# One recurrence, one MLP, one core: an audit of the inputs moved, and a chunk's vector work laid out in other slots

## The chip, the cores and the metric

The kernel runs on one core of a Trainium2 chip. The time is device microseconds of one launch, the median of several runs. The engines are named as in the profile: PE (matrix products), PEld (its weight loads, which overlap), DVE (vector), ACT (scalar functions and copies), POOL (GpSimd), SP (issues the transfers). Each engine takes its instructions in one fixed order; an instruction waits in place for what it needs, and all behind it on that engine wait too.

## The reference

A gated linear recurrence (4 batches, 8 heads, 768 tokens, head size 48), then an MLP with SiLU over the 3072 tokens (384 to 2048 to 384). Attention is float32; the weights come as 64-bit floats, whose bits the kernel converts:

```python
for t in range(S):
    state = alpha[:, :, t, :, None] * state + np.einsum('bhd,bhe->bhde', k[:, :, t], v[:, :, t])
    y[:, :, t] = np.einsum('bhd,bhde->bhe', q[:, :, t], state)
x = y.transpose(0, 2, 1, 3).reshape(B * S, H * D)
h = x @ w_in
out = (h / (1 + np.exp(-h))) @ w_out
```

## The kernel before

**Chunks.** The recurrence is done in chunks of 128 tokens: NT = 24 chunks, n = 0 to 23, four batches for each of six positions in the sequence. Within a chunk it becomes matrix products: with the running products of alpha, k is multiplied by the decay from its token to the chunk's end (`u`, then `kp`), q by the inverse of that (`p`, then `qp`), and scores are masked products of both. A chunk has four stages:

- `products(n)`, lines 648 to 691: alpha, k and q are turned so that the head's dimension lies on the partitions. For the first NA = 8 chunks PE does that (line 669); later DVE does it, with 32x32 transposes (lines 654 to 656) from one set of three tiles ("quads") that twelve transfers fill (lines 461 to 468). DVE scans alpha backwards (line 674), multiplies k (681), takes the chunk's whole decay `c["all"]`, bounds and inverts it (683, 684), scans forwards (686, into `p`, of which there are two) and multiplies q (691).
- `scores(n)`, 693 to 715: PE's scores (702), masked by DVE (706); k is turned back by PE (710) and copied by ACT (712) for the state; from the second position on, DVE multiplies the batch's state by the chunk's decay (715).
- `values(n)`, 720 to 740: y from scores and v, and from q and the state (735), copied by ACT into `xt` (740).
- `states(n)`, 741 to 756: the chunk's addition to the state (PE, 748), summed by DVE (754) or copied at the first position (756). The last position needs none.

The PSUM results of these stages come from one pool of three buffers, `ps_attn()`; 710, 735, 748 and 702 take turns in it.

**The MLP in pieces.** It runs over groups of four chunks (512 tokens), NG = 6. Groups 0 and 1 go through a plain input layer (`enter_plain`, line 791); groups 2 to 5 through `enter` (814), which forms 20 products of sums in place of 24: DVE makes sums of inputs (`sums_x`, eleven per group, 546 to 551) and once sums of weights (`sums_w`, the same lines, made between the pieces of the two output layers named in line 954), ACT copies and applies SiLU (820, 825), DVE combines (828). The output layer (`leave`, 912; 939 for the first one) does seven products in place of eight, with subtractions on DVE (917), sums (926, 977, 979, 988) and stores on SP (928). A generator yields after each piece; a piece of `enter` is twelve matmul records of PE, one of `leave` sixteen. The list `pieces` (1023 to 1040) holds 173 entries in the order in which they are to run, those of a group's input layer in turn with those of the output layer of the group before it.

**The audit** (611 to 640). The scheme holds only for inputs within certain bounds, so the kernel reads alpha (9 transfers of 1024 columns) and the bits of both weight matrices (12 transfers of 512, 16 of 384) a second time, reduces each on DVE (639: one reduction for alpha, two for a weight tile, 65 in all) and compares at the end (1111 to 1125). The generator has one buffer, `look`: a call reduces what the call before it loaded, then issues the next load. If the verdict `within` fails, a general kernel runs behind it (line 1156); all engines load the verdict (1128) and branch.

**What sets the order.** The program is written out by loops of 25 steps of four slots (1086 to 1106): in a slot one stage of one chunk, then `fill`, which calls the audit and runs pieces until the work that is due at that slot is done. A step lasts about as long as PE needs for its pieces. From step 4 on the slots are: scores of the chunk before, products of this chunk, values and states of the chunk before. `load(n + 2)` for the quads stands behind the states. In `fill` the audit is called at every slot while groups 0 and 1 are the ones at work (`i < 2`), at every third slot afterwards: its 37 tiles are all called for by the end of step 24. `settle` (1058) sets up the later chunks' tiles at the end of step 7's second slot.

The written order is a priority, not the last word: a planner orders each engine's instructions by when it expects them to be ready, and the written order decides between those that are. `tc.keep_in_program_order` pins an instruction behind the one that stands ahead of it on its engine in the text; the audit's reductions and the sums of weights are pinned so. Behind attention, 39 of the 173 pieces are left.

Of the kernel before, what the change touches and what calls it, by code (L numbers as in the profile page):

```python
# [8 lines left out]
F32 = mybir.dt.float32  # L9
# [4 lines left out]
ALU = mybir.AluOpType  # L14
# [341 lines left out]
def quotients(  # L356
# [20 lines left out]
    pe, dve, act, gps = nc.tensor, nc.vector, nc.scalar, nc.gpsimd  # L377
    B, H, S, D = q.shape
    C = 128
    NCH = S // C  # L380
    NP = H // 2
# [4 lines left out]
    NT = B * NCH  # L386
    W = C + 1
# [7 lines left out]
    def pool(name, bufs=1, space=None):  # L395
        kw = {} if space is None else {"space": space}
        return ctx.enter_context(tc.tile_pool(name=name, bufs=bufs, **kw))
# [17 lines left out]
    def out_bank(i, n):  # L415
        return outs[i].tile([128, 512], F32, name="ps_o")[:, 0:n]

    def ps_attn(n=C):
        return ps_a.tile([128, 512], F32, name="ps_a").rearrange("p (j c) -> p j c", c=n)
# [18 lines left out]
    NA = 2 * GB  # L438
# [8 lines left out]
    ctxs = {}  # L447

    def load(n):
        c = ctxs.setdefault(n, dict(zip(("ci", "b"), divmod(n, B))))  # L450
        b, rows = c["b"], slice(c["ci"] * C, c["ci"] * C + C)
        for name, src in (("a", alpha), ("k", k), ("q", q)):
            x = src[b, :, rows, :]
            if n < NA:
                c[name] = nat[name][n % NIN]
                nc.sync.dma_start(c[name][:, :, 0:D], x.transpose([1, 0, 2]))
                continue

            c[name] = late["quads"][name]
            for u in range(2):
                for i in range(2):
                    r = 64 * u + 32 * i
                    nc.sync.dma_start(  # L465
                        c[name][r : r + 32, 32 * (1 - i) :][:, 0 : 4 * NP * D].rearrange(
                            "p (g c) -> p g c", g=NP),
                        x[u::2].rearrange("h (b j) d -> b h (j d)", j=4))

    NV = 2  # L470
# [4 lines left out]
    def load_v(n):  # L475
        c = ctxs.setdefault(n, dict(zip(("ci", "b"), divmod(n, B))))
        rows = slice(c["ci"] * C, c["ci"] * C + C)
        t = c["v"] = vns[n % NV]
        nc.sync.dma_start(t[:, :, 0:D], v[c["b"], :, rows, :].transpose([1, 0, 2]))
# [23 lines left out]
    seg = [(fix if i == 0 else spare).tile([128, NP * W + 1], F32, name=f"al{i}") for i in range(2)]  # L503
    inv = fix.tile([128, NP * W + 1], F32, name="inv")
# [137 lines left out]
    xts, xcs, late = {}, {}, {}  # L642

    def tokens(t):

        return t[:, 1 : NP * W + 1].rearrange("p (j c) -> p j c", c=W)[:, :, 0:C]

    def products(n):

        c = ctxs[n]  # L650
        sg, iv = seg[0 if late else n % 2], inv
        ps = {}

        def turned(name, to):
            x = c[name][:, 32:].rearrange("p (g j d) -> p g j d", j=4, d=D)
            dve.transpose(to.rearrange("p g (b j) -> p g j b", j=4), x[:, :, :, 0:32])  # L656

        for name in ("a", "k", "q"):
            if n >= NA:
                if name == "a":  # L660
                    turned(name, tokens(sg))
                continue
            if n < GB and name != "a":

                ps[name] = out_bank("kq".index(name), 512).rearrange("p (j c) -> p j c", c=C)
            else:
                ps[name] = ps_attn()
            for j in range(NP):
                pe.transpose(ps[name][:, j, :], c[name][:, 2 * j : 2 * j + 2, :], ident)
            if name == "a":  # L670
                act.copy(tokens(sg), ps[name])  # L671
        end = NP * W
        u = upool.tile([128, end + 1], F32, name="u")
        dve.tensor_tensor_scan(u[:, end - 1 :: -1], sg[:, end:0:-1], one[:, end:0:-1],  # L674
                               0.0, ALU.mult, ALU.add)

        kp = c["kp"] = u[:, 1 : end + 1].rearrange("p (j c) -> p j c", c=W)[:, :, 0:C]
        if n >= NA:
            ps["k"] = late["turn"].tile([128, NP, C], F32, name="turn")
            turned("k", ps["k"])  # L680
        dve.tensor_tensor(kp, ps["k"], kp, ALU.mult)
        c["all"] = u[:, 0:end:W]
        dve.tensor_single_scalar(least[:, n, :], c["all"], 2.0**-64, ALU.max)
        dve.reciprocal(iv[:, 0:end:W], least[:, n, :])
        p = ppool.tile([128, end + 1], F32, name="p")
        dve.tensor_tensor_scan(p[:, 0:end], sg[:, 0:end], iv[:, 0:end], 0.0, ALU.mult, ALU.add)  # L686
        qp = c["qp"] = tokens(p)
        if n >= NA:
            ps["q"] = late["turn"].tile([128, NP, C], F32, name="turn")
            turned("q", ps["q"])  # L690
        dve.tensor_tensor(qp, ps["q"], qp, ALU.mult)

    def scores(n):
        c = ctxs[n]
        ci, b = c["ci"], c["b"]
        ps = [ps_attn() for _ in range(2)]


        for j in range(NP):
            for u in range(2):  # L700
                r = slice(64 * u, 64 * u + D)
                pe.matmul(ps[u][:, j, :], lhsT=c["kp"][r, j, :], rhs=c["qp"][r, j, :],  # L702
                          start=True, stop=True)
        g = c["g"] = work.tile([128, 2, NP, C], F32, name="g")
        for u in range(2):
            dve.tensor_tensor(g[:, u], ps[u], mask[:, None, :].to_broadcast([128, NP, C]), ALU.mult)  # L706
        if ci < NCH - 1:
            ps_k = ps_attn()
            for j in range(NP):
                pe.transpose(ps_k[:, j, :], c["kp"][:, j, :], ident)  # L710
            c["kn"] = work.tile([128, NP, C], F32, name="kn")
            act.copy(c["kn"], ps_k)
        if ci > 0:
            s = st[b].rearrange("p j u e -> p j (u e)")
            dve.tensor_tensor(s, s, c["all"][:, :, None].to_broadcast([128, NP, 2 * D]), ALU.mult)

# [58 lines left out]
    turn = [0, 1, 2]  # L777
# [267 lines left out]
    def go_on():  # L1045

        nonlocal done
        next(pieces[done][0], None)
        done += 1
# [8 lines left out]
    def settle():  # L1058

        first.close()  # L1060
        late.update(look=pool("look"), part=pool("part"), xc=pool("xc"), turn=pool("turn"),
                    wx=pool("wx").tile([128, 8, NQ, 128], F32, name="wx"))
        quads = pool("quads")
        late["quads"] = {name: quads.tile([128, 32 + 4 * NP * D], F32, name=f"{name}t") for name in "akq"}
        for name, t in late["quads"].items():
            gps.memset(t, 1.0 if name == "a" else 0.0)
        load(NA)

    def fill(step, slot):

        at = step * SLOTS + slot
        if at < marks[0]:
            if step >= 1:
                convert(0, (at - SLOTS) * 3 // (marks[0] - SLOTS) + 1)
            return
        i = next(i for i, m in enumerate(marks[1:]) if at < m)
        a, b = [work_at[n] for n in ([0] + phases)[i : i + 2]]
        due = a + (b - a) * (at - marks[i] + 1) / (marks[i + 1] - marks[i])
        if late and (i < 2 or at % 3 == 0):
            next(audits, None)  # L1080
        while work_at[done + 1] <= due and pieces[done][2] <= bridged:
            convert(0, 3 * (done // 2) + 6)
            convert(1, 3 * (done - 6) // 2)
            go_on()

    for step in range(STEPS):
        stages = ((scores, 1), (products, 0), (values, 1), (states, 1))
        if step < GB:

            stages = stages[1::-1] + stages[2:]  # L1090
        for slot, (stage, lag) in enumerate(stages):
            n = step - lag
            if 0 <= n < NT:
                stage(n)
                if stage is values:
                    bridged = n + 1
                if stage is products and n + NIN < NA:
                    load(n + NIN)
                if stage is states:
                    if NA < n + 2 < NT:  # L1100
                        load(n + 2)
                    if n + NV < NT:
                        load_v(n + NV)
            fill(step, slot)
            if step >= NA - 1 and slot > 0 and conv_done[1] == NFT and not late:
                settle()
    while next(audits, 0) is None:
        go_on()
        go_on()

    checks = [(least.rearrange("p n j -> p (n j)"), ALU.min, 2.0**-64, ALU.is_gt),
              (seen[0][0], ALU.max, 1.0, ALU.is_le)]
# [10 lines left out]
    ps = ps_attn()[0:1, 0, 0:1]  # L1123
# [64 lines left out]
```

## Time and profile before

| | |
|---|---|
| median of 3 runs | 599.41 us (599.15 to 600.26) |
| the profiled execution | 599.32 us |
| its span, first to last instruction | 597.5 us |
| PE busy in it | 570.7 us (96%) |
| DVE busy | 464.0 us (78%) |
| ACT busy | 162.5 us (27%) |
| POOL busy | 7.3 us (1%) |
| moved by DMA | 63.69 MB, 107 GB/s |

Times below and in the prediction are microseconds from the start of the span. A line of the groups gives the source line, the engine, what is written from what, and the count, then busy time and the mean of one in ns, then the engine's idle time ahead of it and what ended that. In a timeline a line is a start and a duration, and in brackets the idle time ahead of it with what ended it. A matmul of float32 is two records of the trace. `seen` is the audit's result, `bits` its buffer (and that of the weights' conversion earlier on), `st` a state, `g` the hidden layer as well as the scores.

### The profile page before, as it was taken

The numbers are of one execution on the slowest core, as the hardware profiler recorded it, in microseconds if no ns is written. First come the engines' busy times: TensorE is split into PE (matmuls) and PEld (weight loads), VectorE is DVE, ScalarE is ACT, GpSimd is POOL, SyncE is SP. The second block draws the span as 40 slices with busy tenths as digits, with TensorE's granted clock in tenths as the row PEclk, the third lists the DMA queues.
The fourth block names the chain that finished last, engine by engine and source line by source line (L and its number), as shares of the span: only waits on it lengthen the run. The fifth ranks groups of instructions, "written<-read, shape, count | busy, mean of one in ns | idle before, by whom it ended". The sixth has DMA issues, their size and how long they took to land.

```text
span 597.5 us, 10662 instructions
## 1 busy us (share of the span) xinstructions
PE 570.7 (96%) x4290; PEld 505.0 (85%) x4290; DVE 464.0 (78%) x835; ACT 162.5 (27%) x279; POOL 7.3 (1%) x25
## 2 busy tenths in 40 slices
PE   5899999988999979989999999999999999999996
PEld 4677887667889868869899999999999998999996
DVE  6889898869999889999699898799794473635531
ACT  2244442011211113123233224223232242342200
POOL 4000000000000000000000000000000000000000
PEclk9999999997999998989999999999999999999999
DMA  9998784346546574343433514333211010000001
GB/s 211 193 239 208 220 199 108 110 131 179 142 142 173 156 180 116 92 126 87 128 84 103 144 49 122 104 93 93 55 54 59 14 35 9 21 7 14 13 21 31
DMA packets 93897, 63.69 MB, mean 107 GB/s; under 512 B 54800, under 2 KB 85520, under 8 KB 93840
## 3 DMA queue, kind: packets, MB, share of 16 engines
q1 hardware_dynamic: 93840, 62.94, 40.8%
q8 instruction: 35, 0.57, 0.4%
q14 instruction: 22, 0.18, 0.1%
HBM read 58.20 MB, written 4.72 MB: 105 GB/s over the span
## 4 chain that ended last, share of the span: by engine, by line
PE 65%; DVE 19%; DMA 10%; issue 2%; SPq 2%; ACT 1%; DVEq 0%; ACTq 0%
PE ps_o L912 27%; PE ps_m L814 20%; PE ps_m L791 5%; PE ps_a L735 4%; DVE seen L639 4%; DMA bits<-in_moe_w_in_dram 3%; PE ps_a L702 3%; PE ps_a L748 2%; DMA bits<-in_alpha_dram 2%; DVE turn L656 2%; DVE u L674 2%; DMA kt<-in_k_dram 1%; PE ps_a L710 1%; DMA at<-in_alpha_dram 1%; SPq L465 1%
## 5 line engine op out<-in xcount | busy, mean ns | idle before, releaser
L912 PE MATMUL ps_o<-w_out,g 128*128 128x192 f32 x704 | 122.5, 328 | 0.2 <-DVE o L926 0.2
L912 PEld LDWEIGHTS ps_o<-w_out,g 128*128 128x128 f32 x704 | 114.8, 190 | 2.9 <-issue 1.0
L791 PE MATMUL ps_m<-xt,w_in 128*128 128x256 f32 x384 | 92.2, 391 | 1.2 <-DVE w_in L604 1.1
L912 PE MATMUL ps_o<-wt,g 128*128 128x192 f32 x528 | 91.2, 326 | 0.0
L912 PEld LDWEIGHTS ps_o<-wt,g 128*128 128x128 f32 x528 | 87.3, 190 | 1.3
L791 PEld LDWEIGHTS ps_m<-xt,w_in 128*128 128x128 f32 x384 | 72.4, 195 | 12.5 <-DVE w_in L604 2.2
L814 PE MATMUL ps_m<-xc,w_in 128*128 128x256 f32 x288 | 70.9, 383 | 2.6 <-DVE g L828 2.6
L814 PEld LDWEIGHTS ps_m<-xc,w_in 128*128 128x128 f32 x288 | 54.4, 192 | 9.3 <-DVE g L828 2.9
L639 DVE TENSOR_REDUCE seen<-bits 128x1 f32<-128x384 int32 (+2 forms) x65 | 42.5, 686 | 14.4 <-DMA bits<-in_alpha_dram 6.7
L917 DVE TENSOR_TENSOR g<-g 128x512 f32<-128x512 f32 x66 | 44.6, 684 | 10.2 <-PE ps_o L912 10.0
L814 PE MATMUL ps_m<-xc,wx 128*128 128x256 f32 x192 | 51.0, 389 | 0.0
L820 ACT COPY g<-ps_m 128x512 f32<-128x512 f32 x64 | 37.6, 587 | 47.8 <-PE ps_m L814 47.8
L825 ACT ACTIVATE g<-g 128x1024 f32<-128x1024 f32 x32 | 33.0, 1055 | 63.6 <-DVE g L828 63.6
L828 DVE TENSOR_TENSOR g<-ps_m,g 128x512 f32<-128x512 f32 x56 | 37.5, 684 | 5.4 <-PE ps_m L814 4.8
L814 PEld LDWEIGHTS ps_m<-xc,wx 128*128 128x128 f32 x192 | 35.6, 193 | 4.9 <-issue 1.2
L794 ACT ACTIVATE g<-ps_m 128x512 f32<-128x512 f32 x32 | 19.1, 598 | 67.1 <-PE ps_m L791 67.1
L674 DVE TENSOR_TENSOR_SCAN u<-al,one 128x516 f32<-128x516 f32 x24 | 29.3, 1225 | 7.0 <-ACT al L671 7.0
L820 ACT COPY part<-ps_m 128x512 f32<-128x512 f32 x32 | 18.8, 587 | 49.1 <-PE ps_m L814 43.6
L706 DVE TENSOR_TENSOR g<-ps_a,mask 128x512 f32<-128x512 f32 x48 | 31.2, 683 | 1.1 <-PE ps_a L702 0.7
L702 PEld LDWEIGHTS ps_a<-p,u 48*128 48x128 f32 x384 | 24.5, 193 | 8.4 <-issue 7.2
L735 PE MATMUL ps_a<-g,vn 128*32 128x128 f32 x768 | 29.4, 285 | 2.1 <-DVE g L706 1.4
L686 DVE TENSOR_TENSOR_SCAN p<-al,inv 128x516 f32<-128x516 f32 x24 | 29.5, 1229 | 2.3 <-PE ps_a L735 1.9
(117 smaller groups left out, 642.1 us busy)
## 6 DMA issues: line engine op xcount, KB each, us to landing
bits<-in_moe_w_in_dram SPq DMA_DIRECT2D x24, 512.0 KB, 4.3
bits<-in_moe_w_out_dram SPq DMA_DIRECT2D x32, 384.0 KB, 3.6
at<-in_alpha_dram SPq DMA_DIRECT2D x64, 96.0 KB, 3.4
kt<-in_k_dram SPq DMA_DIRECT2D x64, 96.0 KB, 3.1
qt<-in_q_dram SPq DMA_DIRECT2D x64, 96.0 KB, 2.9
vn<-in_v_dram SPq DMA_DIRECT2D x24, 192.0 KB, 4.1
bits<-in_alpha_dram SPq DMA_DIRECT2D x9, 512.0 KB, 3.7
out_dram<-o SPq DMA_DIRECT2D x48, 96.0 KB, 1.6
```

Source lines behind the costliest of these rows:

```text
L639: dve.tensor_reduce(seen[kind][which][:, i : i + 1], x, axis=AX, op=op, apply_absolute_value=True))
L674: dve.tensor_tensor_scan(u[:, end - 1 :: -1], sg[:, end:0:-1], one[:, end:0:-1], 0.0, ALU.mult, ALU.add)
L702: pe.matmul(ps[u][:, j, :], lhsT=c["kp"][r, j, :], rhs=c["qp"][r, j, :], start=True, stop=True)
L706: dve.tensor_tensor(g[:, u], ps[u], mask[:, None, :].to_broadcast([128, NP, C]), ALU.mult)
L735: pe.matmul(py[32 * at : 32 * at + 32, t, :], lhsT=w, rhs=x, start=(i < 4), stop=(i >= len(todo) - 4), skip_group_check=True)
L791: pe.matmul(ps[:, e, :], lhsT=w_in[:, t, (f + e) * 128 : (f + e + 1) * 128], rhs=xt[:, t, :], start=(t == 0), stop=(t == NKT - 1))
L814: pe.matmul(ps[:, e], lhsT=block_w(w)[:, 2 * pair + e], rhs=block_x(grp, x), start=(first and e == 0), stop=(e == 1), skip_group_check=True)
L820: act.copy(to, ps)
L825: act.activation(x, x, AF.Silu)
L828: dve.tensor_tensor(to, a, b, op)
L912: pe.matmul(ps, lhsT=x, rhs=w[:, i], start=(first and i == 0), stop=(i == HF - 1), skip_group_check=True)
L917: dve.tensor_tensor(cells(grp, h, pair, *to), cells(grp, h, pair, *x), cells(grp, h, pair, *y), ALU.subtract)
```

## The change

- The audit is called in one slot of four, from step 8 to the end of attention, where it was called in each slot to step 12 and in every third one after that. What is left of it, 20 of the 37 tiles, is called for behind attention, with two pieces and one piece by turns between calls, so over 30 of the 39 pieces that are left; before, no audit was left there. The checks follow, then six pieces as before, then the load of the verdict, and three pieces (33 before).
- From chunk 8 on `products` is cut in two: the scan backwards with the transposes of alpha and k stays in the second slot; a new stage, `quotient`, in the fourth slot, has the inverse, the scan forwards, the transpose of q and its product. For the earlier chunks `products` calls `quotient` at once.
- From step 8 on `states` stands in the third slot, right behind `values`, ahead of that slot's `fill`. The loads of the next chunk's quads follow `quotient` (chunk n + 1 behind n's), in the fourth slot as before.
- The decay of a state is done by ACT, in four instructions of 128x96 with a scale per partition, where DVE did it in one of 128x384.

```diff
@@ -645,20 +645,20 @@
 
         return t[:, 1 : NP * W + 1].rearrange("p (j c) -> p j c", c=W)[:, :, 0:C]
 
+    def turned(x, to):
+        x = x[:, 32:].rearrange("p (g j d) -> p g j d", j=4, d=D)
+        dve.transpose(to.rearrange("p g (b j) -> p g j b", j=4), x[:, :, :, 0:32])
+
     def products(n):
 
         c = ctxs[n]
-        sg, iv = seg[0 if late else n % 2], inv
+        sg = seg[0 if late else n % 2]
         ps = {}
-
-        def turned(name, to):
-            x = c[name][:, 32:].rearrange("p (g j d) -> p g j d", j=4, d=D)
-            dve.transpose(to.rearrange("p g (b j) -> p g j b", j=4), x[:, :, :, 0:32])
 
         for name in ("a", "k", "q"):
             if n >= NA:
                 if name == "a":
-                    turned(name, tokens(sg))
+                    turned(c[name], tokens(sg))
                 continue
             if n < GB and name != "a":
 
@@ -677,18 +677,31 @@
         kp = c["kp"] = u[:, 1 : end + 1].rearrange("p (j c) -> p j c", c=W)[:, :, 0:C]
         if n >= NA:
             ps["k"] = late["turn"].tile([128, NP, C], F32, name="turn")
-            turned("k", ps["k"])
+            turned(c["k"], ps["k"])
         dve.tensor_tensor(kp, ps["k"], kp, ALU.mult)
         c["all"] = u[:, 0:end:W]
+        if n >= NA:
+            c["sg"] = sg
+        else:
+            quotient(n, sg, ps["q"])
+
+    def quotient(n, sg=None, q=None):
+
+        c = ctxs[n]
+        if sg is None:
+            if n < NA:
+                return
+            sg = c.pop("sg")
+        end, iv = NP * W, inv
         dve.tensor_single_scalar(least[:, n, :], c["all"], 2.0**-64, ALU.max)
         dve.reciprocal(iv[:, 0:end:W], least[:, n, :])
         p = ppool.tile([128, end + 1], F32, name="p")
         dve.tensor_tensor_scan(p[:, 0:end], sg[:, 0:end], iv[:, 0:end], 0.0, ALU.mult, ALU.add)
         qp = c["qp"] = tokens(p)
-        if n >= NA:
-            ps["q"] = late["turn"].tile([128, NP, C], F32, name="turn")
-            turned("q", ps["q"])
-        dve.tensor_tensor(qp, ps["q"], qp, ALU.mult)
+        if q is None:
+            q = late["turn"].tile([128, NP, C], F32, name="turn")
+            turned(c["q"], q)
+        dve.tensor_tensor(qp, q, qp, ALU.mult)
 
     def scores(n):
         c = ctxs[n]
@@ -712,7 +725,8 @@
             act.copy(c["kn"], ps_k)
         if ci > 0:
             s = st[b].rearrange("p j u e -> p j (u e)")
-            dve.tensor_tensor(s, s, c["all"][:, :, None].to_broadcast([128, NP, 2 * D]), ALU.mult)
+            for j in range(NP):
+                act.mul(s[:, j], s[:, j], c["all"][:, j : j + 1])
 
 
 
@@ -1076,7 +1090,7 @@
         i = next(i for i, m in enumerate(marks[1:]) if at < m)
         a, b = [work_at[n] for n in ([0] + phases)[i : i + 2]]
         due = a + (b - a) * (at - marks[i] + 1) / (marks[i + 1] - marks[i])
-        if late and (i < 2 or at % 3 == 0):
+        if late and at % 4 == 0:
             next(audits, None)
         while work_at[done + 1] <= due and pieces[done][2] <= bridged:
             convert(0, 3 * (done // 2) + 6)
@@ -1084,29 +1098,34 @@
             go_on()
 
     for step in range(STEPS):
-        stages = ((scores, 1), (products, 0), (values, 1), (states, 1))
+        stages = [[(scores, 1)], [(products, 0)], [(values, 1)], [(states, 1)]]
         if step < GB:
 
             stages = stages[1::-1] + stages[2:]
-        for slot, (stage, lag) in enumerate(stages):
-            n = step - lag
-            if 0 <= n < NT:
+        elif step >= NA:
+            stages = [[(scores, 1)], [(products, 0)], [(values, 1), (states, 1)], [(quotient, 0)]]
+        for slot, group in enumerate(stages):
+            for stage, lag in group:
+                n = step - lag
+                if not 0 <= n < NT:
+                    continue
                 stage(n)
                 if stage is values:
                     bridged = n + 1
                 if stage is products and n + NIN < NA:
                     load(n + NIN)
-                if stage is states:
-                    if NA < n + 2 < NT:
-                        load(n + 2)
-                    if n + NV < NT:
-                        load_v(n + NV)
+                if stage is quotient and n + 1 < NT:
+                    load(n + 1)
+                if stage is states and n + NV < NT:
+                    load_v(n + NV)
             fill(step, slot)
             if step >= NA - 1 and slot > 0 and conv_done[1] == NFT and not late:
                 settle()
+    turns = 0
     while next(audits, 0) is None:
-        go_on()
-        go_on()
+        turns += 1
+        for _ in range(1 + turns % 2):
+            go_on()
 
     checks = [(least.rearrange("p n j -> p (n j)"), ALU.min, 2.0**-64, ALU.is_gt),
               (seen[0][0], ALU.max, 1.0, ALU.is_le)]
```

## The prediction, made before the changed kernel was run

> **What bounds the kernel now.** Three views, in this order: the table by stretches, the waits of TensorE (PE), and the timelines of PE and VectorE (DVE) around each wait. The columns of the table are the stretch and its length, then the busy time of PE, PE's weight loads, DVE, ScalarE (ACT) and POOL, then the granted PE clock.
>
> ```profile
> span 597.5 us, 10662 instructions
> 105.00:210.00 105.00, 100.33 (x820) 83.69 (x818) 92.94 (x161) 16.85 (x33) 0.00 (x0) 0.97 0.53 150
> 210.00:265.00 55.00, 47.58 (x340) 41.99 (x340) 52.41 (x102) 12.54 (x22) 0.00 (x0) 0.94 0.46 120
> 265.00:480.00 215.00, 215.00 (x1727) 196.87 (x1717) 176.36 (x308) 67.47 (x111) 0.00 (x0) 1.00 0.32 86
> 480.00:592.00 112.00, 111.46 (x676) 105.95 (x674) 54.52 (x105) 28.35 (x47) 0.00 (x0) 1.00 0.06 19
> ```
>
> From 265 us on PE never stops, with DVE 82% busy (176.36 / 215). Before that it loses time twice: 105 - 100.33 = 4.67 us and 55 - 47.58 = 7.42 us idle, and a lowered clock, (1 - 0.97) x 105 = 3.15 us and (1 - 0.94) x 55 = 3.30 us. These 18.5 us are all that an order of work can win behind 105 us; the change touches next to nothing ahead of it. In the last stretch PE's 0.54 us is a wait for the check's verdict, and stays. Whom PE waits for from 105 to 500 us (total, times, longest):
>
> ```profile
> PE ps_a L710 <- DVE st L754: 7.2, 2, 3.8
> PE ps_m L814 <- DVE g L828: 3.4, 3, 2.6
> PE ps_a L735 <- DVE g L706: 1.2, 2, 1.1
> PE ps_a L1124 <- DVE good L1122: 0.5, 1, 0.5
> ```
>
> It is always DVE. The longest kind: the transposes of line 710 want a PSUM buffer that the states' sums (line 754) haven't yet emptied. The first of the two, on both engines:
>
> ```profile
> 132.47 1.22 DVE L639 TENSOR_REDUCE seen<-bits 128x1 f32<-128x1024 f32 x1 [2.71 <-DMA bits<-in_alpha_dram]
> 135.61 0.72 DVE L754 TENSOR_TENSOR st<-ps_a,st 48x192 f32<-48x192 f32 x2
> 129.18 2.77 PE L791 MATMUL ps_m<-xt,w_in 128*128 128x256 f32 x12
> 136.47 1.09 PE L710 MATMUL ps_a<-ident,u 128*128 128x128 f32 x4 [3.43 <-DVE st L754]
> 137.35 7.93 PE L791 MATMUL ps_m<-xt,w_in 128*128 128x256 f32 x24
> ```
>
> An audit reduction stood 2.71 us on DVE for its DMA, and the states' sums came behind it. PE idled 3.43 us, and then 24 matmuls took 7.93 us where twelve take 2.77: some 2.4 us more, which is the lowered clock.
>
> The Trainium skill ("TensorE: Matmul & The Clock Gate", section "What's actually happening") says that PE's clock is halved after an idle window of about 3.4 us. By that rule a shorter wait that remains costs its own length only, and the sum below stays; by the rows here it could add up to half of what the two stretches lost to the clock, 3.2 us, and the sum would be 588.0.
>
> **The change part by part.** Steps, slots and pieces are those of the section on the kernel; pieces and audit calls are counted from its loops.
>
> *Audit.*
>
> ```profile
> L639 DVE TENSOR_REDUCE seen<-bits 128x1 f32<-128x384 int32 (+2 forms) x65 | 42.5, 686 | 14.4 <-DMA bits<-in_alpha_dram 6.7 <-DMA bits<-in_moe_w_in_dram 4.6 <-DMA bits<-in_moe_w_out_dram 2.8
> 105.00:210.00 105.00, 21.05 (x25) 0.97 0.53 150
> 210.00:265.00 55.00, 7.11 (x12) 0.94 0.46 120
> ```
>
> Below the group's line is the audit's share of two stretches: 21.05 and 7.11 us of DVE. One call per step leaves about five reductions of 1.22 us in the first stretch (6.1 us) and three in the second (3.7 us), each called a step after its DMA was issued, so that the waits for the DMA (14.4 us in all) go there. The other 20 calls follow behind attention.
>
> *States' decay.*
>
> ```profile
> L715 DVE TENSOR_TENSOR st<-st,u 128x384 f32<-128x384 f32 x20 | 10.8, 542 | 0.0
> L820 ACT COPY g<-ps_m 128x512 f32<-128x512 f32 x64 | 37.6, 587 | 47.8 <-PE ps_m L814 47.8
> L740 ACT COPY xt<-ps_a 128x384 f32<-128x384 f32 x24 | 11.4, 475 | 47.2 <-PE ps_a L735 47.2
> L924 ACT COPY o<-ps_o 128x192 f32<-128x192 f32 x15 | 4.6, 320 | 33.3 <-PE ps_o L912 24.5 <-DMA out_dram<-o 6.9 <-PE ps_o L939 1.9
> ```
>
> It takes 20 x 0.54 us off DVE (six in the first stretch, two in the second: 3.3 and 1.1 us) and puts four instructions of 128x96 on ACT. Copies grow by (587 - 320) / 320 = 0.83 ns per element from 160 ns, so 0.24 us each, about 1 us per chunk. No row shows the scaled form; the bounds are nothing and 4 x 0.32 us. Hidden: ACT works 67.47 of 215 us, and between two uses of a bank by the input layer stands an output piece of PE. If that cover failed, 16 chunks at 0.1 us would cost 1.6 us; I take 0. The Trainium skill ("ScalarE: Activation LUTs", section "What ACT_TABLE_LOAD costs") speaks against it: a scale from a pointer adds 93 ns to 186 ns and 0.833 ns per element, an estimate of 0.36 us each and 1.4 us per chunk, which would change ACT's load and not the sum.
>
> *State products right behind y.* The same eight matmuls and two sums per chunk, one slot earlier, so ahead of the input sums (lines 546 to 551) that share the slot. The buffer that line 710 wants comes free a slot earlier: this and the audit remove the two waits of 7.2 us together.
>
> *Products in two slots.* Nothing is added. Least, reciprocal, second scan, transpose of q and its product move two slots later, behind the states.
>
> ```profile
> 421.40 1.23 DVE L686 TENSOR_TENSOR_SCAN p<-al,inv 128x516 f32<-128x516 f32 x1 [0.95 <-PE ps_a L735]
> 422.66 0.69 DVE L691 TENSOR_TENSOR p<-turn,p 128x512 f32<-128x512 f32 x1
> 429.24 1.16 PE L702 MATMUL ps_a<-p,u 48*128 48x128 f32 x16
> 449.70 1.16 PE L702 MATMUL ps_a<-p,u 48*128 48x128 f32 x16
> ```
>
> The scan waited for its buffer (p has two) until the y two chunks earlier was done, so it is the p that the scores at 449.70 read: 26 us ahead. A step is 449.70 - 429.24 = 20.5 us and two slots half of it, so it stays covered. The next chunk's 12 loads, like before, are queued on SP in the last slot; q's quad comes free later, and is needed a step later. Cost 0, bounds 0 and 10 us (a rival below).
>
> *What is left in the stretches.* First: DVE needs 92.94 - 21.05 + 6.1 - 3.3 = 74.7 us beside PE's 100.33 - 3.15 = 97.2: no wait, DVE comes out without a backlog. Second: 52.41 - 7.11 + 3.7 - 1.1 = 47.9 us beside 47.58 - 3.30 = 44.3: DVE is over by 3.6 us, because the weight sums fall there. I keep 2.5 of them, since PE runs some way ahead of DVE; bounds 0 and 10.7 us (all that it lost there).
>
> *The tail.* Twenty audits over 30 pieces, then the checks, six pieces, the load of the verdict, three pieces. A piece of either layer, the start of three reductions close together, then of three in the loaded stretch:
>
> ```profile
> 502.85 2.59 PE ps_m L814 x12
> 505.44 2.60 PE ps_o L912 x16
> 442.92 1.00 DVE L639 TENSOR_REDUCE seen<-bits 128x1 f32<-128x384 int32 x2
> 446.82 1.01 DVE L639 TENSOR_REDUCE seen<-bits 128x1 f32<-128x384 int32 x2
> 450.63 1.01 DVE L639 TENSOR_REDUCE seen<-bits 128x1 f32<-128x384 int32 x2
> 205.67 1.28 DVE L639 TENSOR_REDUCE seen<-bits 128x1 f32<-128x512 int32 x2 [0.55 <-DMA bits<-in_moe_w_in_dram]
> 210.87 1.28 DVE L639 TENSOR_REDUCE seen<-bits 128x1 f32<-128x512 int32 x2 [0.65 <-DMA bits<-in_moe_w_in_dram]
> 216.50 1.28 DVE L639 TENSOR_REDUCE seen<-bits 128x1 f32<-128x512 int32 x2 [0.34 <-DMA bits<-in_moe_w_in_dram]
> 492.99 1.04 DVE L639 TENSOR_REDUCE seen<-bits 128x1 f32<-128x384 int32 x2 [0.71 <-DMA bits<-in_moe_w_out_dram]
> 494.90 0.15 DVE L1125 TENSOR_SCALAR small<-ps_a 1x1 int32<-1x1 f32 x1 [0.28 <-PE ps_a L1124]
> ```
>
> The audit has one buffer, so a call can't load before the reductions ahead of it: a chain of load and reduction, 3.9 us per audit when all is quiet (446.82 - 442.92). PE's pace allows 30 x 2.6 / 20 = 3.9 us: just enough. DVE has 57 us free in the last stretch and must take about 20 us. Queued behind a reduction that waits are the subtractions of lines 828 and 917, and PE's next piece behind these; a wait of 0.71 us like the one shown hardly reaches PE. I take 1.5 us for twenty of them, bounds 0 and the rival below. The branch at the end is prepared three pieces (7.8 us) ahead instead of 33: 0.
>
> **Sum.** The profiled execution took 599.3 us, of which 597.5 are the span; the median of the runs, 599.41, is the same to 0.02%. 599.3 - 18.5 + 2.5 + 1.5 = 584.8 us.
>
> **Rivals.**
>
> *A, the audit behind attention holds the end (slower).* If the chain runs at the loaded pace, (216.50 - 205.67) / 2 = 5.4 us, twenty take 108 us, the checks 1.9 us more (492.99 to 494.90), and the verdict that PE needs after 36 pieces (93.6 us) is 16.7 us late: 584.8 - 1.5 + 16.7 = 600.0. It begins to cost at 4.6 us per audit and is slower than before from 5.4 us. For it: the stores share SP's queue with the audit's loads, and a store waits there:
>
> ```profile
> SPq L928 <- DVE o L926: 119.4, 30, 11.9
> ```
>
> Against it: those loaded cycles had DMA engines 46% busy, the tail has 6%, and only the first four of the twenty are the larger kind.
>
> *B, DVE still holds the crowded stretch.* The second stretch keeps its 7.42 + 3.30 us, only the first is mended: 599.3 - 7.8 + 1.5 = 593.0. For it: DVE's need there is above PE's. Against: its worst waits stand behind line 754, which moves.
>
> *C, the scores wait for qp.* Where DVE comes to the second half of the products late, PE waits at line 702. At 0.6 us in each of 16 chunks that is 10 us: 595. Against: the 26 us above.
>
> *D, the order does not become what the text says.* The planner lets instructions pass one another, so the waits may merely move: 598 to 599.5. Against: the reductions are pinned behind what is written ahead of them, and they leave the stretches for certain.
>
> **How the numbers follow.** Forecast 0.58 (580 to 590), A 0.13, B 0.14, C 0.07, D 0.08. Predicted 584.8. The range reaches from 579.5 (both remainders nothing, the end's branch 1 us cheaper) to 597.0, over B and C, and leaves out D and most of A: 0.2. About 0.2% (1.2 us) is what a measurement of this kernel can tell from no change. Faster by more: the forecast, B, C and a fifth of A and D, 0.83; within 0.2%: 0.07, most of D; slower: 0.10, most of A.
>
> **What would show it.** Right: no wait of line 710 for line 754; DVE's waits for the audit's DMA gone between 105 and 265 us; clock 1.00 there; the last y about 17 us earlier; a PE busy to its end behind it. Wrong: PE waiting for line 828 where the weight sums run (B), for line 691 (C), or for the verdict, with reductions over 4.6 us apart at the end (A). A wait of over 2 us for ACT anywhere behind 265 us would say that the decay isn't hidden.

## The result, and the profile after

| | before | changed |
|---|---|---|
| median, on one chip by turns | 599.63 us (599.15 to 600.26, 4 runs) | 583.97 us (583.70 to 584.78, 4 runs) |
| ratio, 95% interval | | 0.974 (0.9724 to 0.9757) |
| profiled execution | 599.32 us | 583.70 us |

The change makes the kernel 15.7 us faster. It was forecast as faster, at 584.8 us. The lines of the changed kernel that answer to those of before come first from its table by stretches (stretch, length, busy time of PE, PEld, DVE, ACT and POOL, granted clock, DMA share, GB/s):

```profile
105.00:210.00 105.00, 105.00 (x868) 89.17 (x867) 88.41 (x159) 27.52 (x65) 0.00 (x0) 1.00 0.44 109
210.00:265.00 55.00, 55.00 (x429) 50.11 (x428) 52.53 (x93) 21.37 (x44) 0.00 (x0) 1.00 0.40 108
265.00:465.00 200.00, 200.00 (x1654) 182.70 (x1653) 156.82 (x272) 69.59 (x127) 0.00 (x0) 1.00 0.29 78
465.00:577.00 112.00, 108.14 (x606) 102.00 (x604) 68.64 (x138) 25.82 (x44) 0.00 (x0) 1.00 0.30 89
```

Both stretches that lost time before are full, and the clock is 1.00. In exchange the last one, which had 0.54 us without a matmul before, has 3.86 us. For whom PE waits from 100 us on (total, times, longest):

```profile
PE ps_a L1143 <- DVE good L1141: 1.5, 1, 1.5
PE ps_o L926 <- DVE o L940: 1.1, 1, 1.1
PE ps_o L926 <- DVE u L1002: 0.5, 1, 0.5
```

All three lie behind attention. Line 1143 is the verdict's product (1124 before), 926 the output layer (912), 940 and 1002 its sums (926, 988). The waits of the transposes for the states' sums are gone. How much each part gained and lost is read from two instructions: the last y, and PE's last matmuls. In PE's timeline of the kernel before (start, duration):

```profile
482.72 0.84 PE L735 MATMUL ps_a<-p,st 128*32 128x128 f32 x24
589.32 2.76 PE L912 MATMUL ps_o<-wt,g 128*128 128x192 f32 x16
```

And in that of the changed kernel, with the matmuls behind two of the three waits:

```profile
463.25 0.84 PE L749 MATMUL ps_a<-p,st 128*32 128x128 f32 x24
...
536.62 3.25 PE L926 MATMUL ps_o<-w_out,g 128*128 128x192 f32 x16 [1.14 <-DVE o L940]
539.72 2.76 PE L926 MATMUL ps_o<-wt,g 128*128 128x192 f32 x16
...
561.12 0.19 PE L1143 MATMUL ps_a<-mask,good 128*1 128x1 f32 x2 [1.52 <-DVE good L1141]
...
573.69 2.76 PE L926 MATMUL ps_o<-wt,g 128*128 128x192 f32 x16
```

The last y comes 482.72 - 463.25 = 19.5 us earlier, PE's end 589.32 - 573.69 = 15.6 us earlier. So attention gained 19.5 us and the tail gave 3.8 of them back. Where these went shows in DVE's timeline (in brackets the idle time ahead, and what ended it):

```profile
487.79 1.29 DVE L639 TENSOR_REDUCE seen<-bits 128x1 f32<-128x512 int32 x2 [2.63 <-DMA bits<-in_moe_w_in_dram]
492.83 1.28 DVE L639 TENSOR_REDUCE seen<-bits 128x1 f32<-128x512 int32 x2 [1.25 <-DMA bits<-in_moe_w_in_dram]
497.22 1.01 DVE L639 TENSOR_REDUCE seen<-bits 128x1 f32<-128x384 int32 x2 [0.53 <-DMA bits<-in_moe_w_out_dram]
...
534.10 1.01 DVE L639 TENSOR_REDUCE seen<-bits 128x1 f32<-128x384 int32 x2 [0.47 <-DMA bits<-in_moe_w_out_dram]
535.02 0.68 DVE L842 TENSOR_TENSOR g<-ps_m,g 128x512 f32<-128x512 f32 x1
535.62 0.68 DVE L551 SCALAR_TENSOR_TENSOR g<-g 128x512 f32<-128x512 f32 x1
536.22 0.35 DVE L940 TENSOR_TENSOR o<-ps_o,u 128x192 f32<-128x192 f32 x1
...
558.92 1.01 DVE L639 TENSOR_REDUCE seen<-bits 128x1 f32<-128x384 int32 x2 [2.24 <-DMA bits<-in_moe_w_out_dram]
```

Two things are to be seen. An audit of the larger kind took 492.83 - 487.79 = 5.0 us, one of the smaller (558.92 - 497.22) / 15 = 4.1 us, against the 3.9 us that PE's pace leaves each. And ahead of PE's 1.14 us stands this row of four: a reduction that waited for its load, two instructions of the input layer behind it, and then the sum (line 940) that empties PE's buffer. The groups of the page (busy time, mean ns of one, idle time ahead):

```profile
L729 ACT ACTIVATE st<-st,u 128x96 f32<-128x96 f32 x80 | 25.7, 368 | 51.9 <-DVE u L674 36.8
L639 DVE TENSOR_REDUCE seen<-bits 128x1 f32<-128x384 int32 (+2 forms) x65 | 42.4, 688 | 27.6 <-DMA bits<-in_moe_w_out_dram 21.2
```

The audit is as much work as before (42.4 us), and it stands 27.6 us for its DMA where it stood 14.4. It now does that mostly where DVE has nothing that PE needs soon. The decay is 25.7 us of ACT, 1.29 us for each of 20 chunks.

### The profile page after: what moved, and what is told of

The parts are those of the page before. It is cut to its first block, busy times and chain, and to the rows that moved or that the text cites. A ratio compares the mean times of both kernels' runs of the same rounds, so it can differ in the third digit from the quotient of the medians.

```text
span 582.0 us, 10743 instructions
## 1 busy us (share of the span) xinstructions
PE 564.4 (97%) x4290; PEld 500.4 (86%) x4290; DVE 452.6 (78%) x815; ACT 185.5 (32%) x359; POOL 7.3 (1%) x25
## 5 line engine op out<-in xcount | busy, mean ns | idle before, releaser
L805 PE MATMUL ps_m<-xt,w_in 128*128 128x256 f32 x384 | 88.9, 382 | 1.2 <-DVE w_in L604 1.1
L805 PEld LDWEIGHTS ps_m<-xt,w_in 128*128 128x128 f32 x384 | 70.7, 190 | 11.0 <-DVE w_in L604 2.3
L639 DVE TENSOR_REDUCE seen<-bits 128x1 f32<-128x384 int32 (+2 forms) x65 | 42.4, 688 | 27.6 <-DMA bits<-in_moe_w_out_dram 21.2
L828 PE MATMUL ps_m<-xc,wx 128*128 128x256 f32 x192 | 49.8, 382 | 0.0
L729 ACT ACTIVATE st<-st,u 128x96 f32<-128x96 f32 x80 | 25.7, 368 | 51.9 <-DVE u L674 36.8
L834 ACT COPY part<-ps_m 128x512 f32<-128x512 f32 x32 | 18.8, 587 | 42.4 <-PE ps_m L828 38.1
```

Source lines behind the costliest of these rows:

```text
L639: dve.tensor_reduce(seen[kind][which][:, i : i + 1], x, axis=AX, op=op, apply_absolute_value=True))
L729: act.mul(s[:, j], s[:, j], c["all"][:, j : j + 1])
L805: pe.matmul(ps[:, e, :], lhsT=w_in[:, t, (f + e) * 128 : (f + e + 1) * 128], rhs=xt[:, t, :], start=(t == 0), stop=(t == NKT - 1))
L828: pe.matmul(ps[:, e], lhsT=block_w(w)[:, 2 * pair + e], rhs=block_x(grp, x), start=(first and e == 0), stop=(e == 1), skip_group_check=True)
L834: act.copy(to, ps)
```

## The experiments

Three theories stood against each other: that the audit made the loss and its removal the gain; that the states' new place made it, since every long wait was for line 754; and that it was DVE's load as such, so that whatever is taken off DVE helps alike. The first five kernels do one part alone, or all but one. Ratios are to the kernel before on the same chip, with 95% intervals. The experiments ran on several chips, on which the kernel before took 597.8 to 601.4 us, so the ratios compare across them and the microseconds less well; gains "by the ratio" are shares of 599.6 us.

**The audit alone** (into the kernel before):

```diff
-        if late and (i < 2 or at % 3 == 0):
+        if late and at % 4 == 0:
             next(audits, None)
...
+    turns = 0
     while next(audits, 0) is None:
-        go_on()
-        go_on()
+        turns += 1
+        for _ in range(1 + turns % 2):
+            go_on()
```

> The kernel before with the audit's new spacing alone (one call per step, the other 20 tiles behind attention); decay on DVE, states and products in their old slots. Theory: most of the gain is this part. DVE's waits for the audit's DMA ahead of 265 us go (14 us), and 18 us of reductions with them. In the second stretch DVE needs 49 us beside 44.3 of PE, 1.1 more than with the whole change, and the states' sums still stand behind the input sums, so one wait of line 710 of 1 to 3 us may stay: 585 to 588 us. Rival (the order of the states is what counts): both waits of line 710 stay, 593 us or more.

It took 587.6 us, 0.977 (0.9739 to 0.9801): 13.8 of the 15.7 us, and 11.9 to 15.7 by the interval. Its stretches, and its waits of PE:

```profile
105.00:210.00 105.00, 103.52 (x854) 86.79 (x853) 91.25 (x159) 17.97 (x36) 0.00 (x0) 1.00 0.47 117
210.00:265.00 55.00, 54.86 (x428) 49.89 (x427) 53.84 (x100) 18.42 (x31) 0.00 (x0) 1.00 0.37 96
```

```profile
PE ps_o L912 <- DVE o L926: 1.9, 1, 1.9
PE ps_a L1126 <- DVE good L1124: 1.4, 1, 1.4
PE ps_a L710 <- DVE st L754: 1.1, 1, 1.1
PE ps_a L735 <- DVE g L706: 0.4, 2, 0.2
```

Of 7.2 us of waits for the states' sums one of 1.1 is left, with the states where they always were. The waits of the tail are much like those of the changed kernel. So the audit is the cause of nearly the whole gain and of the loss behind attention.

**All but the audit** (the changed kernel, with the lines above put back as before):

> The changed kernel with the audit as it was before (every slot, then every third; nothing behind attention); decay on ACT, states behind values, products in two slots stay. Theory (the audit is the main cause, the rest adds where DVE's order lets it): the two single parts gained about 3 us each, so 593 to 597 us. Rival (the parts were enough together): 588 us or less.

It took 595.99 us, 0.9968 (0.9944 to 0.9991), 1.9 us by the ratio. And 0.977 x 0.9968 = 0.974: the two halves make up the whole.

**The states alone** (into the kernel before, from step 8; the loads keep their slot by a stage that does nothing else):

```diff
...
+        elif step >= NA:
+            stages = [[(scores, 1)], [(products, 0)], [(values, 1), (states, 1)], [(reload, 0)]]
...
```

> The kernel before with the states right behind the values alone (from step 8); audit as before. Theory (DVE's load and its waits for the audit are the cause): the wait moves from line 710 to another instruction that DVE serves late; 594 to 598 us, a gain of 1 to 5. Rival (order of the states): the 7.2 us of line 710 and about 5 us of lowered clock go, 586 to 588 us.

598.45 us, 0.9957 (0.9931 to 0.9982), 2.6 us by the ratio. The waits of line 710 went, but others came up in their place:

```profile
PE ps_m L814 <- DVE g L828: 4.8, 2, 4.3
PE ps_a L735 <- DVE g L706: 3.1, 4, 1.5
PE ps_a L735 <- issue: 2.0, 1, 2.0
PE ps_m L814 <- DVE xc L550: 1.8, 1, 1.8
```

PE's waits in this view sum to 11.7 us, where those of the kernel before sum to 11.8 (7.2, 3.4 and 1.2): apart from 2.0 us for which the view names no engine, DVE was as late as ever, and only the instruction that PE found unfinished had changed. That takes the second theory away as the main cause.

**The decay alone** (into the kernel before):

```diff
-            dve.tensor_tensor(s, s, c["all"][:, :, None].to_broadcast([128, NP, 2 * D]), ALU.mult)
+            for j in range(NP):
+                act.mul(s[:, j], s[:, j], c["all"][:, j : j + 1])
```

> The kernel before with the states' decay on ACT alone. Theory: 4.4 us less of DVE in the two stretches, no wait for a DMA removed: 596 to 599 us. Rival (DVE's busy time alone is the cause): about as much gained as DVE time removed there, 594.5 us.

598.29 us, 0.9954 (0.9936 to 0.9972): 2.8 us by the ratio, while DVE is late.

**The two slots alone** (`quotient` cut off from `products`, behind the states in the fourth slot):

```diff
...
+        elif step >= NA:
+            stages = [[(scores, 1)], [(products, 0)], [(values, 1)], [(states, 1), (quotient, 0)]]
...
```

> The kernel before with the products in two slots alone (the second half behind the states in the fourth slot). Theory: nothing is added or taken away and the result is 20 us ahead: 598 to 600.5 us. Rival C of the prediction: a wait of line 702 appears, 603 us or more.

599.78 us, 0.9988 (0.9967 to 1.001): no difference that can be told. PE had no wait for `qp`, so this part costs nothing either.

The states and the decay gain 2.6 and 2.8 us alone, but with the slots only 1.9 together. The trace of all but the audit shows one reason. PE's waits (from 100 us on):

```profile
PE ps_m L805 <- ACT g L808: 4.0, 1, 4.0
PE ps_m L828 <- DVE g L842: 3.9, 1, 3.9
PE ps_a L749 <- DVE g L719: 1.1, 1, 1.1
PE ps_m L828 <- ACT kn L725: 0.7, 1, 0.7
```

and ACT's timeline ahead of the first of them:

```profile
142.72 0.37 ACT L729 ACTIVATE st<-st,u 128x96 f32<-128x96 f32 x1 [7.18 <-DVE u L674]
143.00 0.58 ACT L808 ACTIVATE g<-ps_m 128x512 f32<-128x512 f32 x1
```

A decay stood 7.18 us in ACT's order for DVE's scan (line 674), the SiLU of the input layer behind it, and PE behind the SiLU. With DVE late, the decay passes DVE's lateness on to ACT.

**The decay back on DVE** (the changed kernel, with the line of before):

> The changed kernel with the states' decay back on DVE. Theory: with the audit out of the way DVE has 0.54 us per chunk to spare, except where the weight sums fall: 584 to 586 us, a loss of 0 to 2. Rival (the decay on ACT is what keeps the crowded stretch free): waits there, 587 us or more.

585.39 us, 0.9779 (0.9752 to 0.9807). That is 2.3 us by the ratios behind the whole change at 0.974, whose interval (to 0.9757) it just meets. So with the audit out of the way the decay is worth between nothing and some 3 us; these runs don't tell it closer.

**Load, or standing for a load?** The kernel before, its reductions cut to one column, with transfers and order as they are (the rest of the audit is left out):

```diff
-                        dve.tensor_reduce(seen[kind][which][:, i : i + 1], x, axis=AX, op=op,
+                        dve.tensor_reduce(seen[kind][which][:, i : i + 1], x[:, 0:1], axis=AX, op=op,
```

> The kernel before, its audit reducing only the first column of each tile: the rest of the check is left out, the loads and DVE's waits for them stay, 28 us of DVE's busy time ahead of 265 us go. Theory of two causes: the waits stay at 10 us or more and PE still loses in the first stretch: 586 to 593. Rival 1 (DVE's busy time alone): 581 to 584. Rival 2 (the waits for the loads alone): 595 or more.

592.04 us, 0.9853 (0.9831 to 0.9874). Its stretches:

```profile
105.00:210.00 105.00, 99.85 (x822) 84.37 (x820) 76.71 (x163) 16.73 (x33) 0.00 (x0) 0.97 0.57 152
210.00:265.00 55.00, 51.59 (x401) 46.14 (x391) 52.46 (x109) 15.15 (x26) 0.00 (x0) 0.97 0.50 129
```

and DVE's waits in the first of them:

```profile
DVE seen L639 <- DMA bits<-in_moe_w_in_dram: 8.9, 6, 3.4
DVE seen L639 <- DMA bits<-in_alpha_dram: 7.7, 6, 3.5
DVE turn L656 <- DMA kt<-in_k_dram: 6.1, 3, 5.6
```

The same three rows of the kernel before:

```profile
DVE seen L639 <- DMA bits<-in_alpha_dram: 6.7, 4, 2.8
DVE seen L639 <- DMA bits<-in_moe_w_in_dram: 3.6, 4, 1.4
DVE turn L656 <- DMA kt<-in_k_dram: 0.2, 1, 0.2
```

In the first stretch 16 us less work on DVE (76.71 for 92.94) changed nothing for PE: 5.15 us idle for 4.67, the same clock. The time that DVE no longer worked it stood for transfers, 22.7 us for 10.5. The kernel with the audit alone is the counterpart: DVE 91.25 us busy, nearly as before, and PE idle for 1.48. So there it was not the load, but DVE standing for transfers.

Which transfers is another matter. In the kernel before they are the audit's, 10.3 of the 10.5 us. With the short reductions 4.39 of PE's 5.15 us go back to a wait for k's quad. From the chain that ended last (a start and a duration), then from the timelines of DVE and PE:

```profile
143.00 4.06 DMA bits<-in_alpha_dram
147.66 5.13 DMA kt<-in_k_dram
152.87 1.08 DVE L656 STREAM_TRANSPOSE turn<-kt 128x512 f32<-128x512 f32 x1 [5.63 <-DMA kt<-in_k_dram]
157.53 1.09 PE L710 MATMUL ps_a<-ident,u 128*128 128x128 f32 x4 [4.39 <-DVE st L754]
```

The last of k's four transfers was issued at 147.66, on SP right behind an audit load (147.26) that had to wait until the load ahead of it had landed and left the buffer. So the audit's chain of loads holds up two queues, DVE's and SP's. The runs show that this chain is the cause in the first stretch: with the audit alone moved, PE idles 1.48 us there. How much of it reaches PE by DVE's order, by SP's queue, or by transfers that take longer beside the audit's, they don't separate; that it was DVE's order in the kernel before rests on its timeline. In the second stretch the shorter reductions did help (3.41 us idle for 7.42, clock 0.97 for 0.94): there the load was a part of it. The third theory holds for a part of one stretch.

**The price of the tail.** The changed kernel without the audit's loads and reductions (constants stand where its results stood):

> The changed kernel without the audit's loads and reductions: constants stand where its results would be, so that the comparisons at the end still run. It gives the whole price of the audit in the changed kernel. Theory: PE's waits in the tail (1.1 + 0.5 + 1.0 us beyond the half that was there before) and their lowered clock are all of it: 580.5 to 582 us. Rival (the audit's DVE time still costs elsewhere): 579 us or less.

579.4 us, 0.9678 (0.9654 to 0.9703). The audit's whole price in the changed kernel is (0.974 - 0.9678) x 599.6 = 3.7 us, as much as the three waits of the tail, 1.52 + 1.14 + 0.54 = 3.2 us, and 0.5 us for the matmuls that started slowly behind one of them (3.25 us above, beside 2.76). Of 599.6 us the ratio is 580.3, within the theory's range, but its interval just reaches the rival's 579.

**More audits into the tail** (the changed kernel, one call in eight slots, one piece between calls behind attention, so 28 audits over 28 pieces):

```diff
-        if late and at % 4 == 0:
+        if late and at % 8 == 0:
...
-        for _ in range(1 + turns % 2):
+        for _ in range(1):
```

> The changed kernel with the audit called in every second step only, so that 28 tiles instead of 20 are left behind attention, with one piece between calls (28 pieces instead of 30). It puts rival A's case to the test. Theory (through one buffer a tile costs 5.0 us for the first weight matrix and 4.2 for the second): 12 x 5.0 + 16 x 4.2 = 127 us from about 468, so a verdict at 597 where it came at 562 before; PE has 105 us of work there, and waits for the verdict: 602 to 616 us, slower than the kernel before. Rival (PE isn't held by that chain): 582 to 586.

A single execution took 609.65 us, beside 601.25 for the kernel before. PE's timeline at the verdict, and DVE's at the last audit:

```profile
601.16 0.19 PE L1143 MATMUL ps_a<-mask,good 128*1 128x1 f32 x2 [22.36 <-DVE good L1141]
```

```profile
599.50 1.01 DVE L639 TENSOR_REDUCE seen<-bits 128x1 f32<-128x384 int32 x2 [3.12 <-DMA bits<-in_moe_w_out_dram]
```

PE's work leaves 2.6 us for each audit here and the chain of load and reduction takes 4 to 5, so the end waits for it. The slower side that the prediction named (A) is real: it comes with eight audits more behind attention, at one piece each in place of one and a half.

**Loading ahead.** The changed kernel, with the 16 tiles of the second weight matrix loaded by turns into two of the quads' tiles, which are free behind attention, each load issued before the reductions of the tile ahead of it:

```diff
...
+            ahead = kind == 1 and n == HD
+            if last is not None and not ahead:
+                reduced(*last)
+            if ahead:
+                t = late["quads"]["ak"[j % 2]][:, 0 : 2 * n].bitcast(I32)
+                nc.sync.dma_start(t, src.bitcast(I32))
+                x = t.rearrange("p (n w) -> p n w", w=2)[:, :, 1]
...
+            if last is not None and ahead:
+                reduced(*last)
...
```

> The changed kernel, with the 16 tiles of the second weight matrix loaded by turns into two of the quads' tiles, which nothing uses behind attention, and each load issued ahead of the reductions of the tile before. Theory (what the tail loses comes from the chain of load and reduction through one buffer, 4.2 us per audit beside 3.9 of PE): DVE's waits for the second matrix, 21 us, fall below 8, and 1 to 2.5 us of PE's waits go: 581.5 to 583 us. Rival (the reductions' own time on DVE causes PE's waits): no change, 584 us.

578.93 us, 0.9679 (0.9659 to 0.9699), as good as no audit at all and better than expected. DVE's waits for the second matrix (21.2 us) are gone, and the view of PE's waits lists none from 100 us on. In its timeline:

```profile
463.07 0.84 PE L765 MATMUL ps_a<-p,st 128*32 128x128 f32 x24
569.15 2.76 PE L942 MATMUL ps_o<-wt,g 128*128 128x192 f32 x16
```

From the last y to PE's last matmuls are 106.08 us, in the changed kernel 573.69 - 463.25 = 110.44. The one buffer cost 4.4 us: 3.2 are the three waits, 0.5 the slow start, and the rest is not accounted for.

**Both once more, with more rounds on one chip:**

> The changed kernel unaltered, beside the next on the same chip: 0.974 of the kernel before.

> The kernel with the second matrix's audit loaded ahead, again: theory 0.968 of the kernel before, 3 to 4 us under the changed kernel. Rival (the difference was that chip's): no more than 1 us under it.

The changed kernel took 584.41 us, 0.9727 (0.9703 to 0.9751), the one that loads ahead 579.9 us, 0.9653 (0.9636 to 0.9671): 4.5 us less, and faster than both kernels of this case.

## Why the prediction was right

*Where the time was lost: right, and a little too small.* It read 18.5 us out of two stretches ahead of 265 us, all behind DVE. Both are full now, and the last y came 19.5 us earlier, 1.0 more than "all that an order of work can win". The idle time was 12.1 us as read. The surplus is in PE's own work: the matmuls from 105 us to the last y took 365.6 us before and 358.2 after, 7.4 us less, where the lowered clock was put at 6.45; the clock's two decimals alone leave 0.8 us open.

*That the audit is the cause: right, and shown,* by the audit alone (13.8 us). That it is DVE standing for loads and not DVE's load is shown for the first stretch by the shortened reductions, with the reserve made there on which queue stood. For the second stretch it is shown only in part, since there the reductions' time counted too. But the sum by which it cleared the first stretch, 74.7 us of DVE beside 97.2 of PE, was no measure of that. DVE was 88.41 us busy there in the changed kernel, since more of the steps' work falls into the same 105 us (868 PE records for 820), and PE ran all the time.

*The crowded second stretch: mis-sized.* The step "DVE is over by 3.6 us ... I keep 2.5 of them" is the first term that failed. It measured 0: PE lost nothing up to 465 us.

*The tail: mis-sized the other way.* "I take 1.5 us for twenty of them" measured 3.8 us against the kernel before, and 4.4 against the tail that loads ahead. The step behind it was the quiet pace of 3.9 us per audit, just PE's own; from 487.79 to 558.92 us seventeen took 71.1 us, where PE's pace would have needed 17 x 3.9 = 66.3, so the chain fell 4.8 us behind PE. The sign "a PE busy to its end" behind the last y did not come. Also, "a wait of 0.71 us like the one shown hardly reaches PE" overlooked that two instructions can stand between the reduction and the instruction that PE needs. And the wait for the verdict, said to stay at 0.5 us, became 1.5. The two errors, 3.5 us too little gained (19.5 for 18.5 - 2.5) and 2.3 too little given back, largely cancel, which is why 584.8 came within 0.9 us of 583.97: the direction and most of the size are the mechanism's, the closeness of the number is luck.

*The clock: "a shorter wait that remains costs its own length only" doesn't hold.* With the audit alone a wait of 1.91 us was followed by a clock of 0.63 (last section). The sum was spared, since from 100 us on no wait in the changed kernel's profile is longer than 1.52 us; the 3.2 us that the prediction set against this sentence measured 0.

*The decay on ACT: hidden, as said, at half as much again per instruction.* "0.24 us each" measured 0.368. The Trainium skill's estimate of 0.36 ("ScalarE: Activation LUTs", section "What ACT_TABLE_LOAD costs"), given beside it, was the better one: its price for a scale from a pointer is in this trace. The sum didn't hang on it, since no wait for ACT exists behind 100 us. Not foreseen was that the decay can hand DVE's lateness on (4.0 us in all but the audit).

*The states, the slots and the branch: right in kind.* States and audit were said to remove the two waits together; the audit alone does nearly all of it. The slots measured nothing. From the start of PE's last matmuls to the span's end are 597.5 - 589.32 = 8.2 us before and 582.0 - 573.69 = 8.3 us after, so the branch prepared late costs nothing.

*The rivals.* B fell (no wait for line 842, which was 828, and none in the second stretch). C fell (no wait for `qp`, with the slots alone neither). D fell for the whole, but describes well what the states alone do: there the waits moved. A came only in small, as the verdict's 1.5 us, and is the nearest of them: the audit's pace stood at 4.1 to 5.0 us, around the 4.6 from which it was to cost, and 28 audits over 28 pieces made it come true. Two sums of the prediction are off by 0.1 and 0.3 us, without effect: A's lateness comes to 16.6 us, the lower end of the range to 579.8.

## What to carry to other kernels

A check that runs beside the work on an engine with a fixed order can cost more by the time it stands there for its data than by its own work: call it so seldom that its load has always landed, or load ahead. Its loads also stand in the queue of the engine that issues them, and what is queued behind them there comes late as well. Before such a chain is moved behind the busy part, its cycle with one buffer (load and reduction, one after the other) is to be set against the pace of the engine that sets the end, with the margin in view; buffers that the finished part leaves free take the load out of the cycle. When a wait is removed by moving the instruction that it names, look whether the engine is still late: then the wait only gets another name.

## What the runs showed of the hardware

Short waits cost PE more than their length. Behind one of 1.14 us in the changed kernel the next sixteen matmuls took 3.25 us for 2.76, though the row of that stretch (busy time of PE, granted clock, DMA share, GB/s) gives the clock as granted in full:

```profile
536.60:539.80 3.20, 3.06 (x17) 1.00 0.35 127
```

What slows the first matmuls then, no run here shows. Behind a wait of 1.91 us, in the kernel with the audit alone, the clock itself was lowered, and sixteen took 4.62 us:

```profile
541.59 4.62 PE L912 MATMUL ps_o<-w_out,g 128*128 128x192 f32 x16 [1.91 <-DVE o L926]
541.60:546.20 4.60, 4.60 (x17) 0.63 0.43 126
```

The Trainium skill's rule ("TensorE: Matmul & The Clock Gate", section "What's actually happening") has the clock lowered after an idle window of about 3.4 us. The row behind 1.14 us agrees with it, the one behind 1.91 us does not. Over the traces of all the kernels here, from 105 us on, the clock was below 1.00 in the 3 us behind each of the sixteen waits of PE that lasted 1.79 us or more, and at 1.00 behind each of the seventeen from 1.05 to 1.76 us, up to the next wait.
